# Where the combined weights are made and when the fourth batch's loads are queued, in a one-core attention and mixture kernel

## The chip, the cores and the metric

The kernel runs on one core of a Trainium2 chip. The metric is the device time of one execution in microseconds (us), lower is better. Engines are called as in the profile: PE is TensorE's matrix multiply and PEld its weight load, DVE is VectorE, ACT is ScalarE, POOL is GpSimd, and SP is SyncE, whose queue issues every DMA of this kernel.

## What is computed

Four batches of 576 tokens go through a block-causal attention with 8 heads of 64, then through a first network, in which the largest of three products is taken per element, then through four experts whose outputs are weighted by shares and added:

```python
attn = softmax(where(block_i >= block_j, q @ k.T / 8, -1e9)) @ v       # 4 x 8 heads x 576 x 64
x = attn as 2304 tokens x 512
h = max(max(x @ w1, x @ w2), x @ w3)                                   # 512 -> 768
x = h @ w_out                                                          # 768 -> 512
p = domain_probs / sum(domain_probs)                                   # 2304 x 4, the shares
out = sum over e of p[:, e] * (relu(x @ w1[e]) @ w2[e])                # 512 -> 1024 -> 512
```

Each product is made of three matmuls on pairs of a rounded value and its remainder, so that it is near float32.

## The kernel before, in words

**Order of the work.** The attention runs over 16 pairs of heads, four pairs to a batch. The first network of batches 0, 1 and 2 (`moe1`, L545) is a generator that the class `Filler` (L686) steps in between the steps of the attention of the batch behind it: so many of its matmuls are put behind each attention step. When the attention ends, 15 or 16 steps of batch 2's network are left. Then come batch 3's network in another form (`moe1_last`, L577) and the experts (from L1351).

**First network.** `moe1` takes 18 weight tiles (`order`, L551; three weight matrices, six tiles of 128 hidden columns each), 12 matmuls for each, into one PSUM bank; ACT (L560) or DVE (L562) evicts it. Its second layer, `moe1_out` (L535), runs over four output tiles d; each needs a weight tile "wo" of 768 KB that `moe_weight` (L462, DMA at L475) loads from `held`, where batch 0 left the weights as pairs. There are two buffers of "wo", so the tile of d = 2 can come only when the matmuls of d = 0 are over, and that of d = 3 when those of d = 1 are.

**Combined weights.** Batch 3 forms each product of 2 x 2 blocks from seven block products instead of eight, nine groups of seven (`moe1_last`, L597 to 681). Four of the seven need sums of weight blocks. These are made ahead by `sums` (L517), in batches 1 and 2, as soon as both tiles of a group have been used: two additions (L523), four more (L525 to 528), a rounded copy on ACT (L529), a difference (L530), all in a part of `arena` as scratch, and a DMA of 1 MB to `summed[g]` (L531). Groups 0 to 3 are made in batch 1, groups 4 to 8 in batch 2 (`SHARE = 4`), all in the same part of `arena`, that of batch 2's outputs: a group's first addition waits for the store of the group before. `moe1_last` loads them (L611) into the tiles "xh", "xl" and two buffers of "w1", in turn. The "w1" buffers lie where the attention's tiles lay.

**Shares.** Twelve small DMAs (L794 four, L802 eight) load the expert shares into `pr`, four small DVE instructions (L804 to 807) make `prt` of them. They stand in the code right behind the end of the attention. `keep_in_program_order` queues each of them behind the SP instruction that stands before it in the code.

**Expert weights.** `weights_in(e, n)` (L960) loads raw first-layer weights into the one scratch tile "t" (L968), combines them on DVE (L936) and splits them into pairs on ACT and DVE (L944) in a buffer of "w1". `combine` (L841) uses the same "t" for the token blocks. `save_tails` (L880) stores token blocks (L885) for a later pass.

**What sets the order.** Code order is not queue order. The framework's planner simulates the engines and each queue, and puts into a queue what its simulation holds for ready, the earlier in the code the sooner. On the chip each queue then runs strictly in that order: an instruction that waits holds up all behind it. `tc.issue_after(ins)` adds an edge for what is traced within it and runs on the same engine as `ins`: it is queued behind `ins`, and doesn't wait for its end.

The end of the stage, in code order (L1292 to 1309):

```python
    filler.work.append(moe1_last(xc))
    for _ in following:
        filler.upto(filler.done + 1)
    while begun[0] < NGRP - 1:
        filler.upto(filler.done + 1)
    ready = [weights_in(0, 0)]
    filler.upto(filler.done + 8)
    following = combine(*blocks(0))
...
    ready.append(weights_in(0, 1))
    filler.rest()
    save_tails()
```

Of the kernel before, what the change touches and what calls it, by code (L numbers as in the profile page):

```python
# [7 lines left out]
F32R = mybir.dt.float32r  # L8
# [4 lines left out]
ALU = mybir.AluOpType  # L13
AX = mybir.AxisListType
# [3 lines left out]
RAWS = 3  # L18

WT = 5  # L20
SHARE = 4
FROM = 8
P = 128

# [4 lines left out]
def program(tc, q, k, v, w123, w_out, probs, e_w1, e_w2, out):  # L29
    nc = tc.nc  # L30

    B, H, D, S = k.shape[0], 2 * k.shape[1], k.shape[2] // 2, k.shape[3]
    NT, DM = out.shape
    FF = w_out.shape[2] // 2
    E, F2 = e_w1.shape[0], 2 * P * e_w1.shape[1]
    KD = DM // P
    NF = FF // P
    NPAIR = H // 2
    NTT = NT // P
# [4 lines left out]
    def f(ap):  # L44
        return ap.bitcast(F32)
# [5 lines left out]
    prs = const.tile([P, NTT], F32, name="prs")  # L51
# [3 lines left out]
    prt = const.tile([P, E, NTT], F32, name="prt")  # L55
# [10 lines left out]
    summed = [dram.tile([P, 2, 4, 2 * P], F32, name=f"summed{i}") for i in range(3 * NF // 2)]  # L66
# [18 lines left out]
    CT, KH = 384, KD // 2  # L85
# [12 lines left out]
    pairs, later, made, exps, normal, least = {}, [], {}, [], [], []  # L98
# [363 lines left out]
    def moe_weight(b, n, at=0, a0=0):  # L462

        if b == 0:
            return convert.weight(n)
        A = tiles[n].shape[1]
        wide = n >= 3 * NF
        if b == B - 1 and not wide:
            if at == 0:
                taken[0] = 0  # L470
            if at % WT >= 3:
                wide = True
                taken[0] += 1
        wt = weight_tile(n, wide)
        nc.sync.dma_start(  # L475
            out=f(wt[:, :, a0:A].rearrange("p k a f -> p k (a f)")), in_=held[n][:, :, a0 * P:A * P]
        )
        return wt
# [37 lines left out]

    def sums(g, w0, w1):  # L517

        o = 2 * KD * S
        high, raw = (arena[:, o + i * 8 * P:o + (i + 1) * 8 * P] for i in range(2))  # L520
        for i, w in enumerate((w0, w1)):
            x = [w[:, j].rearrange("p a f -> p (a f)") for j in range(2)]
            nc.vector.tensor_tensor(raw[:, i * 4 * P:(i + 1) * 4 * P], f(x[0]), f(x[1]), op=ALU.add)  # L523
        a11, a12, a21, a22 = (raw[:, i * 2 * P:(i + 1) * 2 * P] for i in range(4))
        nc.vector.tensor_tensor(a22, a21, a22, op=ALU.add)  # L525
        nc.vector.tensor_tensor(a21, a11, a21, op=ALU.subtract)
        nc.vector.tensor_tensor(a11, a22, a11, op=ALU.subtract)
        nc.vector.tensor_tensor(a12, a12, a11, op=ALU.subtract)
        nc.scalar.copy(high.bitcast(F32R), raw)  # L529
        nc.vector.tensor_tensor(raw.bitcast(F32R), raw, high, op=ALU.subtract)  # L530
        nc.sync.dma_start(  # L531
            out=summed[g].rearrange("p x s f -> p (x s f)"), in_=arena[:, o:o + 16 * P]
        )

    def moe1_out(b, runs):  # L535
        for d in range(KD):
            wt = moe_weight(b, 3 * NF + d)
            for w, hh, hl, to in runs:
                m = ps_m.tile([P, 512], F32, name="m", tag="m")[:, 0:w]
                yield from mm3(m, [(wt[:, 0, ff], wt[:, 1, ff], hh[ff], hl[ff]) for ff in range(NF)])  # L540
                x = to(d)
                nc.scalar.copy(x, m if len(x.shape) == 2 else m.rearrange("p (b s) -> p b s", b=B))
                yield

    def moe1(b):  # L545
        hidden = [mp.tile([P, NF, MAIN], F32R, name=x, tag=x) for x in ("hh", "hl")]
        hh, hl = ([x[:, ff] for ff in range(NF)] for x in hidden)
        xh, xl = xs[b]
        prev, last = {}, {}
        if b:  # L550
            order = [(2 * j + i, n) for j in range(NF // 2) for n in range(3) for i in range(2)]  # L551
        else:
            order = [(ff, n) for ff in range(NF) for n in range(3)]
        for at, (ff, n) in enumerate(order):
            wt = moe_weight(b, 3 * ff + n, at)
            m = ps_m.tile([P, 512], F32, name="m", tag="m")[:, 0:MAIN]
            yield from mm3(m, [(wt[:, 0, d], wt[:, 1, d], xh[:, d], xl[:, d]) for d in range(KD)])
            if n == 0:
                prev[ff] = mp.tile([P, MAIN], F32, name="mt", tag="mt", bufs=3)
                nc.scalar.copy(prev[ff], m)  # L560
            else:
                nc.vector.tensor_tensor(prev[ff], m, prev[ff], op=ALU.max)  # L562
            t = prev[ff]
            if n == 2:
                nc.gpsimd.tensor_scalar(hh[ff], t, 1.0, 0.0, op0=ALU.mult, op1=ALU.add)
                nc.gpsimd.tensor_tensor(hl[ff], t, f(hh[ff]), op=ALU.subtract)
            if b and ff % 2:
                g = 3 * (ff // 2) + n
                if (g >= SHARE) == (b > 1):
                    sums(g, last[0], wt)  # L570
            last[0] = wt
            yield
        yield from moe1_out(b, [(MAIN, hh, hl, lambda d: x2f[b][:, d, 0:MAIN])])

    begun = [0]

    def moe1_last(xc):  # L577

        b = B - 1
# [13 lines left out]
            nc.vector.tensor_tensor(to, x, y, op=ALU.add)  # L593
            return to

        at = 0
        for j in range(NF // 2):  # L597
            state = {}
            for n in range(3):
                begun[0] += 1  # L600
                w0 = moe_weight(b, 6 * j + n, at)
                w1 = moe_weight(b, 6 * j + 3 + n, at + 1, KH)
                at += 2
                tag = ("xh", "xl", "w1", "w1")[(3 * j + n) % 4]
# [3 lines left out]
                else:  # L608
                    w2 = mp.tile([P, KD, MAIN], F32R, name=tag, tag=tag).rearrange("p d (s f) -> p (d s) f", s=2)
                w2 = w2.rearrange("p (x s) f -> p x s f", x=2)  # L610
                nc.sync.dma_start(  # L611
                    out=f(w2).rearrange("p x s f -> p (x s f)"),
                    in_=summed[3 * j + n].rearrange("p x s f -> p (x s f)"),
                )

                def side(name, x, k):
                    if name in TERMS:
# [85 lines left out]
    filler = Filler()  # L703
# [24 lines left out]
    for n in range(NALL):  # L728
        b, d = divmod(n, NPAIR)
# [45 lines left out]
    def rows(p, c, t):  # L775
        if p < NPASS - 1:
            return [(0, (2 * p + c) * S + t * P, P)]
        found, at = [], t * P
        while at < (t + 1) * P:
            b, s = divmod(at, TAIL)  # L780
            n = min((t + 1) * P - at, TAIL - s)
            found.append((at - t * P, (2 * c + b) * S + CT + s, n))
            at += n
        return found

    def tile_of(p, c, t):
        return (2 * p + c) * TPC + t

    pr = xp.tile([P, NTT, E], F32, name="pr", tag="pr")
    for p in range(NPASS):  # L790
        for c in range(2):
            if p < NPASS - 1:
                r0 = (2 * p + c) * S
                tc.keep_in_program_order(nc.sync.dma_start(  # L794
                    out=pr[:, tile_of(p, c, 0):tile_of(p, c, TPC)],
                    in_=probs[r0:r0 + CT].rearrange("(t p) e -> p t e", p=P),
                ))
                continue
            for t in range(TPC):
                for a, r, n in rows(p, c, t):  # L800
                    tc.keep_in_program_order(
                        nc.sync.dma_start(out=pr[a:a + n, tile_of(p, c, t)], in_=probs[r:r + n])  # L802
                    )
    nc.vector.tensor_reduce(prs, pr, axis=AX.X, op=ALU.add)  # L804
    nc.vector.tensor_scalar(prs, prs, 1e-9, None, op0=ALU.add)
    nc.vector.reciprocal(prs, prs)
    nc.vector.tensor_tensor(
        prt.rearrange("x e t -> x t e"), pr, prs[:].unsqueeze(2).to_broadcast([P, NTT, E]), op=ALU.mult
    )
    shares = dram.tile([E * NTT, P], F32, name="shares")  # L810

    def split(dst_h, dst_l, raw, low):
# [67 lines left out]
    def save_tails():  # L880
        for d in range(2):
            for c in range(2):
                x = tokens(NPASS - 1, c, d)
                for k in range(KH):
                    nc.sync.dma_start(out=tails[d][c][:, k], in_=x[:, k])  # L885
# [71 lines left out]
    def load(out_, in_):  # L957
        loads.append(nc.sync.dma_start(out=out_, in_=in_))

    def weights_in(e, n):  # L960

        w = xp.tile([P, 7, 2, QW_], F32R, name="w1", tag="w1", bufs=2)
        if (e, n) in stored:
            load(f(w[:]), kept1[e][n][:])
            return w
        stored.add((e, n))
        raw = scratch()[:, 0:7 * QW_].rearrange("x (n f) -> x n f", n=7)
        nc.sync.dma_start(out=raw[:, 0:4], in_=e_w1[e, n])  # L968
        combos(*(raw[:, i] for i in (0, 1, 2, 3, 4, 5, 6, 3)))
        halves(w, raw, [(nc.vector, 0, 4), (nc.vector, 4, 7)])  # L970
        nc.sync.dma_start(out=kept1[e][n][:], in_=f(w[:]))
        return w
# [321 lines left out]
    filler.work.append(moe1_last(xc))  # L1294
    for _ in following:
        filler.upto(filler.done + 1)
    while begun[0] < NGRP - 1:
        filler.upto(filler.done + 1)
    ready = [weights_in(0, 0)]
    filler.upto(filler.done + 8)  # L1300
    following = combine(*blocks(0))
    xc = next(following)
    for _ in following:
        filler.upto(filler.done + 3)
    ready.append(weights_in(0, 1))
    filler.rest()
    save_tails()
    moe.close()
    ps.close()
# [180 lines left out]
```

## Time and profile before

| what | value |
|---|---|
| time, median of 3 runs | 1244.34 us (1242.67 to 1246.34) |
| time of the profiled execution | 1241.92 us |
| its span, first to last instruction | 1240.1 us |
| PE busy | 1191.9 us, 96% of the span |
| DVE, ACT, POOL busy | 903.8, 486.0, 283.4 us |
| attention with batches 0 to 2 | from 0 to about 391 us |
| batch 3's network, its second layer to the end | about 412 to 512 us |
| experts | 512 to 1240 us |

A row of the timeline has the start, the duration, the engine and line, what it writes and reads, and in brackets how long its engine was idle before it and what ended that. A window's row has for each engine the busy time and the number of instructions, then PE's granted clock (1.00 is 2.4 GHz, 0.50 is 1.2 GHz), the busy share of the DMA engines and GB/s. "SPq" rows are DMAs as SP issues them; the time from issue to landing is told separately.

### The profile page before, as it was taken

The page shows a single profiled execution, that of the slowest core. Times are in us where ns is not written, and L with a number is a line of the kernel's source. Part 1 is how long each engine was busy: PE and PEld are TensorE (multiplying, and loading weights), DVE is VectorE, ACT ScalarE, POOL GpSimd, SP SyncE. Part 2 cuts the span into 40 slices and gives each one's busy share as a digit, 9 for nine tenths or more (in the row PEclk, how much of TensorE's full clock was granted, in tenths as well). Part 3 has the DMA queues.
Part 4 walks back from the last instruction along what each step waited for, and adds up shares of the span by engine and source line. Part 5 has one row for each costly group of instructions (what it writes and reads, how often), then busy time and mean ns, then how long its engine had stood idle before and what let it go on. Part 6 is the DMA issues. An engine that isn't in the chain of part 4 may idle for free.

```text
span 1240.1 us, 18286 instructions
## 1 busy us (share of the span) xinstructions
PE 1191.9 (96%) x6887; PEld 1069.8 (86%) x6887; DVE 903.8 (73%) x1570; ACT 486.0 (39%) x1008; POOL 283.4 (23%) x300
## 2 busy tenths in 40 slices
PE   7889999999997998999999999999999999999998
PEld 4567777777775897889999998999999999999998
DVE  4877876554665467598888896758787888686896
ACT  5976664445335123344444450233232223322232
POOL 2459754433332000233333341000000000000000
PEclk8999999999999899899999999999999999999999
DMA  5846766744556564788888865867888887766754
GB/s 207 278 139 218 249 205 215 237 144 138 164 179 218 182 213 160 269 314 320 311 320 303 302 236 175 309 253 314 317 304 310 315 314 280 255 256 232 254 204 178
DMA packets 84652, 303.51 MB, mean 245 GB/s; under 512 B 8973, under 2 KB 20565, under 8 KB 69461
## 3 DMA queue, kind: packets, MB, share of 16 engines
q1 hardware_dynamic: 84564, 302.35, 68.5%
q8 instruction: 54, 0.88, 0.3%
q14 instruction: 34, 0.27, 0.1%
HBM read 209.75 MB, written 92.57 MB: 244 GB/s over the span
## 4 chain that ended last, share of the span: by engine, by line
PE 66%; DVE 14%; DMA 11%; ACT 5%; issue 2%; POOL 1%; SPq 0%; DVEq 0%; ACTq 0%; POOLq 0%
PE m L993 20%; PE o L1152 17%; PE m L489 13%; PE m L625 5%; DMA t<-in_e_w 4%; PE tt L286 2%; PE pv L321 2%; PE st L188 2%; DMA summed<-arena 2%; ACT p L232 2%; PE m L1152 2%; DVE w L948 2%; DVE hl L1054 2%; DMA part<-in_e_w 1%; DVE tmp L1013 1%
## 5 line engine op out<-in xcount | busy, mean ns | idle before, releaser
L993 PE MATMUL m<-t,w 128*128 128x384 f32 x1152 | 227.9, 336 | 1.3 <-DVE w L948 1.3
L1152 PE MATMUL o<-hx,w 128*128 128x384 f32 x1176 | 226.1, 337 | 0.5 <-DMA w<-kb 0.5
L1152 PEld LDWEIGHTS o<-hx,w 128*128 128x128 f32 x1176 | 207.9, 188 | 0.8 <-PE m L993 0.8
L993 PEld LDWEIGHTS m<-t,w 128*128 128x128 f32 x1152 | 203.4, 188 | 4.2 <-DVE w L948 1.6
L993 PE MATMUL m<-b,w 128*128 128x384 f32 x864 | 175.4, 336 | 1.5 <-ACT tmp L1018 1.5
L993 PEld LDWEIGHTS m<-b,w 128*128 128x128 f32 x864 | 153.1, 188 | 4.9 <-ACT tmp L1018 1.8
L232 ACT ACTIVATE p<-st,mn 128x128 f32<-128x128 f32 (+2 forms) x144 | 78.7, 557 | 71.6 <-DVE mn L225 71.3
L258 POOL TENSOR_SCALAR p<-p,sm 128x128 f32<-128x128 f32 (+4 forms) x108 | 78.0, 737 | 103.9 <-ACT high L126 51.2
L948 POOL TENSOR_TENSOR w<-part,w 128x512 fp32r<-128x512 f32 x32 | 50.1, 1587 | 192.5 <-ACT w L946 192.4
L1013 DVE TENSOR_TENSOR tmp<-m,tmp 128x384 f32<-128x384 f32 x144 | 77.5, 550 | 17.3 <-PE m L993 14.6
L489 PE MATMUL m<-xh,wt 128*128 128x512 f32 x256 | 85.6, 399 | 0.0
L489 PE MATMUL m<-hh,wo 128*128 128x512 f32 x192 | 67.5, 419 | 13.7 <-DMA wo<-held 12.1
L1123 ACT CAST hx<-hq 128x768 fp32r<-128x768 f32 x49 | 40.6, 837 | 99.0 <-PE o L1152 76.1
L225 DVE TENSOR_REDUCE mn<-st 128x1 f32<-128x128 f32 (+2 forms) x144 | 68.1, 512 | 15.3 <-ACT p L232 7.3
L286 PE MATMUL tt<-ident,p 128*128 128x128 f32 x400 | 62.7, 289 | 15.1 <-ACT eh L296 6.6
L1079 PE MATMUL o<-w,hl 128*128 128x512 f32 x192 | 74.7, 391 | 0.0
L1078 PE MATMUL o<-w,hh 128*128 128x512 f32 x192 | 74.6, 390 | 0.0
L1075 PE MATMUL o<-w,hh 128*128 128x512 f32 x192 | 74.3, 391 | 0.0
L286 PEld LDWEIGHTS tt<-ident,p 128*128 128x128 f32 x400 | 48.0, 147 | 29.8 <-ACT eh L296 8.2
L948 POOL TENSOR_TENSOR part<-mix,part 128x512 fp32r<-128x512 f32 x32 | 44.1, 1385 | 75.7 <-ACT part L946 75.7
L1123 ACT CAST hx<-part 128x768 fp32r<-128x768 f32 x28 | 23.3, 836 | 91.4 <-PE o L1152 69.4
L489 PEld LDWEIGHTS m<-hh,wo 128*128 128x128 f32 x192 | 38.0, 200 | 24.1 <-issue 6.8
(225 smaller groups left out, 2275.6 us busy)
## 6 DMA issues: line engine op xcount, KB each, us to landing
w<-kb SPq DMA_DIRECT2D x55, 1024.0 KB, 5.9
w<-ka SPq DMA_DIRECT2D x28, 1792.0 KB, 7.6
ka<-w SPq DMA_DIRECT2D x16, 1792.0 KB, 6.7
kb<-part SPq DMA_DIRECT2D x16, 1024.0 KB, 6.6
wt<-held SPq DMA_DIRECT2D x28, 512.0 KB, 4.7
kb<-w SPq DMA_DIRECT2D x16, 768.0 KB, 5.5
arena<-in_w SPq DMA_DIRECT2D x18, 512.0 KB, 4.6
wo<-held SPq DMA_DIRECT2D x12, 768.0 KB, 5.5
```

The lines of the kernel that those rows point to most:

```text
L225: least.append(nc.vector.tensor_reduce(mn[:, m:m + 1], x, axis=AX.X, op=ALU.min))
L232: exps.append(nc.scalar.activation(to, x, ACTF.Exp, bias=mn[:, m:m + 1], scale=-1.0, accum_out=sm[:, m:m + 1],))
L258: normal.append(nc.gpsimd.tensor_scalar(x, x, sm[:, c:c + 1], 1.0, op0=ALU.mult, op1=ALU.mult))
L286: nc.tensor.transpose(tt[:, c:c + P], pt[i][:, k0:k0 + P], ident)
L489: nc.tensor.matmul(out=out_, lhsT=w, rhs=x, start=m == 0, stop=m == n - 1)
L948: eng.tensor_tensor(w[:, a:b, 1], raw[:, a:b], f(w[:, a:b, 0]), op=ALU.subtract)
L993: ins = nc.tensor.matmul(out=m, lhsT=a, rhs=b, start=start and n == 0, stop=stop and n == 3 * KH - 1, skip_group_check=True,)
L1013: nc.vector.tensor_tensor(t, x, y, op=ALU.add)
L1075: ins = nc.tensor.matmul(out=o, lhsT=hh[:, ts], rhs=wh, start=i == 0, stop=False)
L1078: nc.tensor.matmul(out=o, lhsT=hh[:, ts], rhs=wl, start=False, stop=False)
L1079: nc.tensor.matmul(out=o, lhsT=hl[:, ts], rhs=wh, start=False, stop=i == G - 1)
L1152: nc.tensor.matmul(out=o, lhsT=a, rhs=b, start=start and m == 0, stop=stop and m == 2, skip_group_check=True,)
```

## The change

Four things. `sums` makes the even groups in batch 1 (five: 0, 2, 4, 6, 8) and the odd ones in batch 2 (four), and groups 2 and 6 use another part of `arena`, that of batch 1's outputs. `sums` becomes a generator in two halves: the additions come where they came, and the copy, the difference and the store are traced behind the next weight tile's eviction, the copy under `issue_after` of it. The loads of combined weights into "w1" are queued behind the last weight load of batch 2 (`made["load"]`, its fourth "wo"). The loads of the shares are traced once six groups of batch 3 have begun, and queued behind the sixth group's load of combined weights; the first load of expert weights is queued behind the last such load traced by then (the eighth group's), and the second, `weights_in(0, 1)`, is traced behind all of batch 3 and queued behind its last "wo" load.

```diff
-SHARE = 4
...
         wt = weight_tile(n, wide)
-        nc.sync.dma_start(
+        made["load"] = nc.sync.dma_start(
...
     def sums(g, w0, w1):
 
-        o = 2 * KD * S
+        o = (2 - (g // 2 % 2) * (g % 2 == 0)) * KD * S
...
-        nc.scalar.copy(high.bitcast(F32R), raw)
+        behind = yield
+        with tc.issue_after(behind.ins):
+            nc.scalar.copy(high.bitcast(F32R), raw)
         nc.vector.tensor_tensor(raw.bitcast(F32R), raw, high, op=ALU.subtract)
         nc.sync.dma_start(
             out=summed[g].rearrange("p x s f -> p (x s f)"), in_=arena[:, o:o + 16 * P]
         )
+        yield
...
             if n == 0:
                 prev[ff] = mp.tile([P, MAIN], F32, name="mt", tag="mt", bufs=3)
-                nc.scalar.copy(prev[ff], m)
+                ins = nc.scalar.copy(prev[ff], m)
             else:
-                nc.vector.tensor_tensor(prev[ff], m, prev[ff], op=ALU.max)
+                ins = nc.vector.tensor_tensor(prev[ff], m, prev[ff], op=ALU.max)
+            if under:
+                under.pop().send(ins)
...
             if b and ff % 2:
                 g = 3 * (ff // 2) + n
-                if (g >= SHARE) == (b > 1):
-                    sums(g, last[0], wt)
+                if g % 2 == b - 1:
+                    under.append(sums(g, last[0], wt))
+                    next(under[0])
             last[0] = wt
             yield
+        for x in under:
+            x.send(ins)
...
-        at = 0
+        at, behind = 0, made["load"]
...
-                nc.sync.dma_start(
-                    out=f(w2).rearrange("p x s f -> p (x s f)"),
-                    in_=summed[3 * j + n].rearrange("p x s f -> p (x s f)"),
-                )
+                with tc.issue_after(behind.ins) if tag == "w1" else nullcontext():
+                    made["sums"] = nc.sync.dma_start(
+                        out=f(w2).rearrange("p x s f -> p (x s f)"),
+                        in_=summed[3 * j + n].rearrange("p x s f -> p (x s f)"),
+                    )
...
+    def load_shares():
+        for p in range(NPASS):
...
+        nc.vector.tensor_reduce(prs, pr, axis=AX.X, op=ALU.add)
...
-    def weights_in(e, n):
+    def weights_in(e, n, behind=None):
...
-        nc.sync.dma_start(out=raw[:, 0:4], in_=e_w1[e, n])
+        with tc.issue_after(behind.ins) if behind else nullcontext():
+            nc.sync.dma_start(out=raw[:, 0:4], in_=e_w1[e, n])
...
+    while begun[0] < 6:
+        filler.upto(filler.done + 1)
+    with tc.issue_after(made["sums"].ins):
+        load_shares()
     while begun[0] < NGRP - 1:
         filler.upto(filler.done + 1)
-    ready = [weights_in(0, 0)]
+    ready = [weights_in(0, 0, made["sums"])]
...
-    ready.append(weights_in(0, 1))
     filler.rest()
+    ready.append(weights_in(0, 1, made["load"]))
     save_tails()
```

`load_shares` holds the loops and the four DVE instructions of L790 to 809 unchanged.

## Rows read from the trace of the kernel before

**Rows 1.** Windows: engines' busy time (instructions), granted clock, DMA share, GB/s.

```profile
core 0: us, PE busy (x) PEld busy (x) DVE busy (x) ACT busy (x) POOL busy (x), PEclk, DMA share, GB/s
...
202.40:205.80 3.40, 3.40 (x9) 2.67 (x8) 2.04 (x1) 0.65 (x2) 2.49 (x2) 0.50 0.35 96
206.00:232.00 26.00, 25.98 (x166) 20.23 (x166) 17.61 (x39) 10.71 (x29) 7.94 (x9) 1.00 0.67 228
...
326.00:379.00 53.00, 48.65 (x288) 37.46 (x286) 37.30 (x81) 21.58 (x58) 20.77 (x23) 1.00 0.61 216
399.60:403.80 4.20, 0.00 (x0) 0.00 (x0) 1.91 (x6) 1.42 (x2) 0.00 (x0) 1.00 0.37 84
403.80:410.60 6.80, 4.83 (x11) 3.80 (x12) 2.23 (x5) 0.00 (x0) 0.00 (x0) 0.50 0.51 181
492.30:495.90 3.60, 0.00 (x0) 0.00 (x0) 1.31 (x4) 0.69 (x3) 0.00 (x0) 1.00 0.96 350
495.90:502.80 6.90, 5.42 (x13) 4.26 (x14) 2.30 (x3) 1.69 (x2) 0.00 (x0) 0.51 1.03 410
512.00:530.00 18.00, 18.00 (x106) 17.68 (x105) 15.10 (x21) 9.21 (x17) 9.76 (x7) 1.00 0.72 257
```

**Rows 2.** Timeline of PE, 200 to 500 us.

```profile
201.39 0.50 PE L489 MATMUL m<-xh,wu 128*128 128x512 f32 x1 [1.87 <-ACT mt L560]
...
395.11 0.62 PE L489 MATMUL m<-hh,wo 128*128 128x512 f32 x2
...
405.77 0.77 PE L489 MATMUL m<-hh,wo 128*128 128x512 f32 x1 [6.20 <-DMA wo<-held]
...
436.25 1.20 PE L625 MATMUL m<-b,wo 128*128 128x384 f32 x6
...
497.38 0.80 PE L489 MATMUL m<-hh,wo 128*128 128x512 f32 x1 [5.13 <-DMA wo<-held]
```

**Rows 3.** Queue of SP: DMAs as they are issued, 391 to 500 us.

```profile
391.11 0.81 SPq L611 DMA_DIRECT2D w<-summed  x2
391.97 3.55 SPq L794 DMA_DIRECT2D pr<-in_probs  x4
395.57 5.63 SPq L802 DMA_DIRECT2D pr<-in_probs  x8
401.31 1.03 SPq L475 DMA_DIRECT2D wo<-held  x2
...
427.73 0.33 SPq L611 DMA_DIRECT2D xl<-summed  x1
430.18 2.60 SPq L475 DMA_DIRECT2D wo<-held  x2
...
490.13 0.33 SPq L968 DMA_DIRECT2D t<-in_e_w  x1
...
491.82 1.01 SPq L475 DMA_DIRECT2D wo<-held  x2
```

**Rows 4.** Chain of work that ended last, in order of time: start, us, what.

```profile
401.31 4.33 DMA wo<-held
...
491.82 5.52 DMA wo<-held
```

**Rows 5.** Time from issue to landing of the "wo" loads, 290 to 520 us.

```profile
DMA to landing us min/median/max: 3.8/4.7/10.9
```

**Rows 6.** SP's waits, 463 to 516 us: total, times, longest.

```profile
SPq L475 <- PE m L489: 0.5, 1, 0.5
```

**Rows 7.** Timeline of DVE: the sums of group 1, and weights of expert 0.

```profile
193.90 1.29 DVE L523 TENSOR_TENSOR arena<-wu 128x512 f32<-128x512 f32 x2 [3.80 <-DMA summed<-arena]
...
496.89 2.09 DVE L948 TENSOR_TENSOR w<-t,w 128x1024 fp32r<-128x1024 f32 x2 [0.78 <-ACT w L946]
```

**Rows 8.** Waits, 180 to 405 us: total, times, longest.

```profile
DVE arena L523 <- DMA summed<-arena: 17.4, 7, 4.2
...
ACT arena L529 <- DVE arena L528: 24.1, 5, 8.3
```

More of the change, by code (lines that the diff above doesn't have):

```diff
@@ L548, in moe1 @@
         xh, xl = xs[b]
-        prev, last = {}, {}
+        prev, last, under = {}, {}, []
         if b:
@@ L789, in program @@
     pr = xp.tile([P, NTT, E], F32, name="pr", tag="pr")
[L790 to L809, printed above, removed]
+    def load_shares():
+        for p in range(NPASS):
+            for c in range(2):
+                if p < NPASS - 1:
+                    r0 = (2 * p + c) * S
+                    tc.keep_in_program_order(nc.sync.dma_start(
+                        out=pr[:, tile_of(p, c, 0):tile_of(p, c, TPC)],
+                        in_=probs[r0:r0 + CT].rearrange("(t p) e -> p t e", p=P),
+                    ))
+                    continue
+                for t in range(TPC):
+                    for a, r, n in rows(p, c, t):
+                        tc.keep_in_program_order(
+                            nc.sync.dma_start(out=pr[a:a + n, tile_of(p, c, t)], in_=probs[r:r + n])
+                        )
+        nc.vector.tensor_reduce(prs, pr, axis=AX.X, op=ALU.add)
+        nc.vector.tensor_scalar(prs, prs, 1e-9, None, op0=ALU.add)
+        nc.vector.reciprocal(prs, prs)
+        nc.vector.tensor_tensor(
+            prt.rearrange("x e t -> x t e"), pr, prs[:].unsqueeze(2).to_broadcast([P, NTT, E]), op=ALU.mult
+        )
     shares = dram.tile([E * NTT, P], F32, name="shares")
```

## The prediction

> **What bounds the kernel now.** I read first the windows, stage by stage: PE is the engine that is full nearly everywhere (25.98 of 26 us from 206 to 232, 18.00 of 18 from 512), so a change pays only where PE is idle or its clock is low. In the stages touched the windows show three such places [rows 1]. From 399.6 PE does nothing for 4.2 us and then runs at a granted clock of 0.50 (1.2 GHz) until 410.6. From 492.3 to 495.9 it does nothing again, then runs at 0.51 until 502.8. From 202.4 to 205.8 it runs at 0.50. And between 326 and 379 it is busy 48.65 of 53.00 us.
>
> PE's timeline says what each idle stretch waited for [rows 2]: 6.20 us before 405.77 and 5.13 us before 497.38 for a "wo" weight tile, 1.87 us before 201.39 for an ACT eviction. SP's queue tells why the first tile was late [rows 3]: two "w" loads at 391.11, then twelve loads of shares from 391.97 to 401.2, and only then "wo", at 401.31. Its buffer was free much earlier: the matmuls of the tile before it ended with the first one of the pair at 395.11, at about 395.5 [rows 2]. So the wait is SP's own order. The chain of waits carries both loads, 4.33 and 5.52 us [rows 4].
>
> **The second layer of batch 2.** The shares leave this place, and the "w" loads are queued behind the "wo" load. Then "wo" can be issued at 395.5 instead of 401.31. It lands 4.33 us later [rows 4], the other landings lying between 3.8 and 10.9 [rows 5]; I take 4.33, the same load at the same place, with now less ahead of it. That gives 399.9, and PE is done with its other work at 405.77 - 6.20 = 399.57. Of the 6.20 us some 0.4 remain. The half clock goes too: PE was busy 4.83 us at 0.50 [rows 1], of which 2.4 were lost. Gain 6.2 + 2.4 - 0.4 = **8.2 us**. Bounds: with the slowest landing (10.9) 1.6, with the fastest 8.6. Nothing else is late next that I see: the products behind have their operands, whose last preparation on DVE stood behind the shares' own loads.
>
> **The second layer of batch 3.** The load of expert weights at 490.13 (512 KB) moves behind the two "wo" loads at 491.82 [rows 3]. But SP was not what held these: its only wait for PE there is 0.5 us [rows 6], it was there when the buffer came free. So the issue time stays; only the landing can shrink, from 5.52 to the 4.33 of the load with little traffic beside it [rows 4]: 1.2 us. The clock had fallen 3.6 us after the last matmul here and 4.2 us after it in the other place [rows 1]; an idle stretch of 5.1 - 1.2 = 3.9 us lies between these, so I count no gain from it. Gain **1.2 us**; bounds 0 (same landing) and 1.2 + 2.7, half of the 5.42 us at 0.51 [rows 1], if the clock holds.
>
> **The sums in batch 1.** Group 1 goes to batch 2, and group 2 uses another buffer. DVE waited 3.80 us at 193.90 for group 0's store before it began group 1 [rows 7]; behind it stood the reductions that ACT's exponentials wait for, behind these the eviction that PE waited for at 201.39 [rows 2]. That wait goes: 1.87 us, and of the 3.40 us at 0.50 [rows 1] half, 1.7. Gain **3.6 us**; bounds 0, if group 0's second half, now behind an eviction, gets in the same way, and 3.6. The batch has one group more to make (five, not four). From 206 to 232, where two groups were made within 26 us with such waits, PE lost 0.02 us [rows 1], so I cost the further ones at nothing; their cover is the matmuls of batch 1, and the rival below prices its failing.
>
> **The sums in batch 2.** Four groups instead of five, every fourth weight tile instead of every second, so the store of one is over before the next begins. DVE's waits for such stores are 17.4 us in seven times over both batches, ACT's waits for DVE's additions 24.1 us in five [rows 8]. PE's idle time from 326 to 379 is 53.00 - 48.65 = 4.35 us [rows 1]. I take 3.0 of it, as the rest is the attention's own chain; bounds 0 and 4.35. The moved copy costs ACT nothing new, it is the same copy later; SP's stores move with it, to places where no load was waiting long.
>
> **The shares.** Their twelve issues fall behind the sixth load of combined weights, at 427.73 in the old times [rows 3]. Behind them in the queue is the "wo" load of the fifth group, free at 430.18, first used at 436.25 [rows 2, 3]; landing at 4.7 [rows 5], it has about 1.4 us to spare. The planner looks at each load when it is ready, so some four shares go ahead of it and delay it by part of one issue. I take 0.3; bounds 0 and, if all twelve go first, 427.73 + 0.33 + 9.2 + 0.3 + 4.7 = 442.2, a PE wait of 6.0 us and half a clock behind it as at 405.77, 2.4: 8.4. DVE's four instructions take under 1 us where DVE has room.
>
> **The expert weights.** The first load goes behind the eighth sums load; its buffer came free later than that anyway. The second lands about 5 us later, and with it the difference at 496.89 [rows 7]. These weights serve the second seven products of the experts: the first take 42 of the 106 matmuls that fill 18.00 us from 512 [rows 1], so until 519. From 499 + 5 to 519 leaves 15 us. But the scratch tile and the third load go 5 us later too. I take 0.5; bounds 0 and 5.
>
> A page of the Trainium skill speaks against these two moves: DMA: Bandwidth & Descriptors, Rules for kernel authors, wants a DMA issued early and its semaphore waited for late. By it the full 5 us would be lost, and the sum below would come to 1231.2. By the trace the issue that matters is one that something waits for, and the shares were early and cost 6.2 us to the tile behind them.
>
> **Sum.** 8.2 + 1.2 + 3.6 + 3.0 - 0.3 - 0.5 = 15.2 us. The profiled execution took 1241.92 us, which gives 1226.7. The median of the runs is 2.4 us above it; the sum from that is 1229.1. I say **1228**. About 0.3%, 3.7 us, is what a measurement of this kernel can tell from no change. The forecast's own range is 1222 to 1234.
>
> **Rivals.** *The shares block the group's weights.* All twelve are queued ahead of the fifth group's "wo": 8.4 us instead of 0.3, so 1234.8. For it: only about 1.4 us to spare. Against: before, they stood ahead because they stood earlier in the code, and now they stand behind that load. Chance 0.10.
>
> *The sums wait elsewhere.* The order behind the eviction binds only where that eviction is ACT's: issue order holds on one engine, and two of three evictions are DVE's. Then ACT still waits for DVE's additions, PE gains nothing in batches 1 and 2 and keeps 15.2 - 6.6 = 8.6: 1233.3. For it: the 24.1 us of such waits [rows 8]. Against: longer distances leave less to wait for. Chance 0.12.
>
> *Late expert weights.* PE waits for them once at the start of the experts, 5 us: 1231.2. Chance 0.03, as 15 us lie between.
>
> *Slower: the extra sums stop the attention.* Five groups in batch 1, each additions and difference on DVE in front of the reductions, each costing PE what group 1 did at 201.39, 3.6 us. That stretch has no idle time now, so it is all loss: four more such stops are 14.4 us, the one of before stays, batch 2 gains nothing. From 8.2 + 1.2 - 0.8 = 8.6 us of gain follows a loss of 5.8: 1247.7. It decides from the third stop on. For it: one such stop is in the trace. Against: it needed the wait for a store, and the two groups after it, with waits, cost nothing. Chance 0.10.
>
> *It doesn't do what it says.* The "wo" load of batch 2 is again not first in the queue, as another load is held for ready there, and the gain of 8.2 falls to about 1, with the sums' gain lost to the planner's new order: 1240 to 1244. Chance 0.08. Against: an edge now holds the "w" loads behind it.
>
> **How the numbers follow.** The forecast has 0.57, the rivals 0.10, 0.12, 0.03, 0.10 and 0.08. Faster by over 0.3% (below 1240.6): 0.57 + 0.10 + 0.12 + 0.03 = 0.82. Within: 0.08. Slower: 0.10. The last two rivals are 0.18, left out, so the range ends at 1240; below, the clock at 497 (2.7), all of 4.35 in batch 2 and the two small costs at zero would add 4.9 to the sum of the profile, 1221.8, and with the new planning order something more: 1219.
>
> **What would show it.** In the profile of after: "wo" issued at about PE's end of the tile before it, with no loads of shares around it, and no window at 0.50 near 400; the wait before batch 3's third "wo" still there, about 4 us; no wait of DVE for a store of sums; no gap before the eviction near 200; PE idle under 1.5 us where it had 4.35; the shares scattered among loads of batch 3 with PE full. Wrong would make it: a PE wait for "wo" in the fifth group, new gaps in batch 1, or PE waiting for expert weights after 512.

## The result, and the profile after

The changed kernel takes 1229.25 us (median of four runs, 1227.60 to 1229.60); the kernel before, run beside it, 1243.51 (1241.37 to 1246.34). The ratio is 0.9881, 95% interval 0.9858 to 0.9904: faster by 1.2%, against 1228 forecast. The profiled execution took 1227.60 us with a span of 1225.8.

Where the time went is read from four points that every version's PE timeline has: a wait for a converted "wo" in batch 0, the attention's last wait in batch 2, the first of batch 3's products, and the experts' first. Of the kernel before:

```profile
172.41 0.50 PE L489 MATMUL m<-hh,wo 128*128 128x512 f32 x1 [0.88 <-ACT wo L101]
388.23 0.87 PE L321 MATMUL pv<-eh,vraw 128*64 128x384 f32 x4 [0.73 <-ACT eh L296]
412.23 1.22 PE L625 MATMUL m<-b,wt 128*128 128x384 f32 x6
512.51 1.21 PE L993 MATMUL m<-b,w 128*128 128x384 f32 x6
```

Of the changed kernel, the same points and, between them, its long waits, which answer to [rows 2]:

```profile
171.44 0.50 PE L488 MATMUL m<-hh,wo 128*128 128x512 f32 x1 [0.88 <-ACT wo L100]
213.42 1.09 PE L285 MATMUL tt<-ident,p 128*128 128x128 f32 x8 [1.22 <-POOL p L257]
282.07 0.56 PE L488 MATMUL m<-hh,wo 128*128 128x512 f32 x1 [4.19 <-DMA wo<-held]
383.69 0.87 PE L320 MATMUL pv<-eh,vraw 128*64 128x384 f32 x4 [0.73 <-ACT eh L295]
395.25 0.50 PE L488 MATMUL m<-hh,wo 128*128 128x512 f32 x1 [0.21 <-DMA wo<-held]
399.49 1.21 PE L633 MATMUL m<-b,wt 128*128 128x384 f32 x6
482.86 0.80 PE L488 MATMUL m<-hh,wo 128*128 128x512 f32 x1 [4.55 <-DMA wo<-held]
497.50 1.21 PE L1004 MATMUL m<-b,w 128*128 128x384 f32 x6
505.24 0.51 PE L1086 MATMUL o<-w,hh 128*128 128x512 f32 x1 [1.19 <-ACT w L956]
506.88 1.35 PE L1004 MATMUL m<-t,w 128*128 128x384 f32 x5 [1.13 <-DVE tmp L1024]
```

The stop at 201.39 [rows 2] has no counterpart, and of the 6.20 us before 405.77 there are 0.21 left, before 395.25. One of 4.19 us at 282.07 is new, and so are two small ones in batch 1, that at 213.42 and one of 0.87 us at 242.06. The points cut each span into five stages, and each stage's length is a difference of two rows (the last ends with the span). Gains over the kernel before, in us, one profiled execution each:

| stage | length before | forecast | changed kernel |
|---|---|---|---|
| 1, to batch 0's "wo" | 172.41 | 0 | 1.0 |
| 2, sums beside the attention | 215.82 | 6.6 | 3.6 |
| 3, second layer of batch 2 | 24.00 | 8.2 | 8.2 |
| 4, batch 3 | 100.28 | 1.2 - 0.3 | 2.3 |
| 5, experts | 727.59 | -0.5 | -0.7 |

Stage 1 has the same code in every version and is 168.83 to 173.42 us long in the fourteen profiles; its 1.0 is chance, not a gain of the change. Stages 2 to 5 give 13.3 us.

The windows of the changed kernel, which answer to [rows 1]:

```profile
core 0: us, PE busy (x) PEld busy (x) DVE busy (x) ACT busy (x) POOL busy (x), PEclk, DMA share, GB/s
277.80:282.10 4.30, 0.11 (x2) 0.04 (x1) 1.33 (x3) 4.30 (x13) 1.78 (x3) 1.00 1.00 332
282.10:285.80 3.70, 3.70 (x9) 2.89 (x10) 0.00 (x0) 0.05 (x1) 2.01 (x3) 0.54 0.33 136
322.00:374.00 52.00, 52.00 (x346) 41.20 (x344) 31.60 (x71) 23.49 (x65) 20.85 (x28) 1.00 0.50 169
396.00:406.00 10.00, 10.00 (x54) 9.34 (x54) 2.08 (x3) 2.57 (x5) 0.00 (x0) 1.00 0.59 226
482.90:487.20 4.30, 4.30 (x10) 3.43 (x11) 0.25 (x1) 0.00 (x0) 0.00 (x0) 0.50 0.90 290
500.00:512.00 12.00, 9.67 (x45) 8.98 (x44) 10.25 (x17) 6.11 (x11) 5.68 (x4) 0.86 0.58 197
```

Where PE was idle for 4.35 us from 326 to 379, its counterpart is full, 52.00 of 52. The half clock near 400 is gone (1.00 from 396), that after batch 3's wait is still there (0.50), and a third has come at 282 (0.54), behind the new wait.

The chain of waits has three "wo" loads now, the first of them new (the others answer to [rows 4]):

```profile
275.77 6.25 DMA wo<-held
...
390.99 4.21 DMA wo<-held
...
478.10 4.71 DMA wo<-held
```

SP's queue in batch 3, answering to the shares of [rows 3]: they go out in portions between the other loads, and "wo" gets its place among them.

```profile
415.34 2.03 SPq L803 DMA_DIRECT2D pr<-in_probs  x4
417.46 0.53 SPq L474 DMA_DIRECT2D wo<-held  x1
418.04 2.33 SPq L811 DMA_DIRECT2D pr<-in_probs  x3
420.47 0.56 SPq L474 DMA_DIRECT2D wo<-held  x1
421.07 2.87 SPq L811 DMA_DIRECT2D pr<-in_probs  x5
```

The waits, as in [rows 8]: DVE's for stores of sums no longer appear (17.4 us before); ACT's for DVE's additions are fewer.

```profile
ACT arena L530 <- DVE arena L527: 14.7, 3, 5.6
```

**The new wait.** Group 1 is now batch 2's first group. Its additions need only its two weight tiles, which are loaded ahead, so the planner places them before batch 1's second layer. The timelines of DVE and ACT, in order of time, then SP's queue, then SP's waits there:

```profile
266.60 0.69 DVE L522 TENSOR_TENSOR arena<-wt 128x512 f32<-128x512 f32 x1 [2.80 <-DMA wt<-held]
...
272.96 1.05 ACT L530 CAST arena<-arena 128x1024 fp32r<-128x1024 f32 x1 [4.97 <-DVE arena L527]
...
274.05 1.27 DVE L531 TENSOR_TENSOR arena<-arena 128x1024 fp32r<-128x1024 f32 x1 [0.52 <-ACT arena L530]
```

```profile
266.65 0.33 SPq L114 DMA_DIRECT2D vraw<-in_v  x1
275.35 0.33 SPq L532 DMA_DIRECT2D summed<-arena  x1
275.77 2.45 SPq L474 DMA_DIRECT2D wo<-held  x2
```

```profile
SPq L532 <- DVE arena L531: 8.3, 1, 8.3
```

DVE's additions run from 266.60 to 272.9, with batch 2's inputs in between; ACT's copy waited for them, the difference for the copy, and SP for 8.3 us for the difference, with batch 1's third "wo" next in the queue. This reading was a guess until the third run below.

### The profile page after: what moved, and what is told of

Read it like the earlier page. It is cut to its first block, busy times and chain, and to the rows that moved or that the text cites. A ratio compares the mean times of both kernels' runs of the same rounds, so it can differ in the third digit from the quotient of the medians.

```text
span 1225.8 us, 18284 instructions
## 1 busy us (share of the span) xinstructions
PE 1186.1 (97%) x6887; PEld 1068.0 (87%) x6887; DVE 901.4 (74%) x1570; ACT 486.1 (40%) x1008; POOL 285.3 (23%) x300
## 4 chain that ended last, share of the span: by engine, by line
PE 85%; DMA 5%; ACT 4%; DVE 3%; POOL 2%; issue 1%; SPq 0%; POOLq 0%; DVEq 0%; ACTq 0%
PE m L1004 28%; PE o L1163 17%; PE m L488 14%; PE m L633 5%; PE o L1090 4%; PE o L1089 4%; PE o L1086 4%; PE tt L285 3%; PE st L187 2%; PE pv L320 2%; PE m L1163 2%; ACT p L231 2%; DMA wo<-held 1%; DMA w<-kb 1%; DMA wu<-held 1%
## 5 line engine op out<-in xcount | busy, mean ns | idle before, releaser
L1135 DVE TENSOR_TENSOR hx<-hq,hx 128x768 fp32r<-128x768 f32 x49 | 46.6, 953 | 16.0 <-ACT hx L1134 15.7
```

## The experiments

Twelve versions were timed, 5 to 12 executions of each. The intervals are about 0.2% to either side, some 2.5 us, so smaller differences between versions are read from the stages of the profiles. That is one execution of each version, and not always a typical one: what stages 2 to 5 gain together and what the ratio says differ by 0.4 to 2.5 us, and by 4.8 in one version (store and tails). In the names "t" is the load of raw expert weights, "kb" the store of converted second-layer weights for a later pass, and a room is one of a tile's buffers. Gains over the kernel before, in us:

| version | ratio (95% interval) | stage 2 | 3 | 4 | 5 |
|---|---|---|---|---|---|
| changed kernel | 0.9881 (0.9858 to 0.9904) | 3.6 | 8.2 | 2.3 | -0.7 |
| loads only | 0.9952 (0.9934 to 0.9969) | -0.7 | 8.1 | 2.2 | -3.1 |
| sums only | 0.9967 (0.9951 to 0.9982) | 3.2 | 0.3 | 0.0 | -1.2 |
| group 1's store behind "wo" | 0.9855 (0.9836 to 0.9873) | 9.5 | 8.4 | 2.9 | -1.4 |
| expert weights at the old place | 0.9906 (0.9884 to 0.9927) | 4.2 | 8.1 | -0.4 | -2.3 |
| shares at the old place | 0.9884 (0.9868 to 0.9901) | 3.7 | 8.4 | 1.9 | -1.3 |
| without the w1 edge | 0.9936 (0.9915 to 0.9956) | 1.3 | 7.3 | 2.5 | -5.7 |
| the same, kb behind t | 0.9913 (0.9893 to 0.9933) | 3.6 | 6.8 | 2.7 | -0.9 |
| copy at once | 0.9913 (0.9891 to 0.9935) | 3.1 | 8.2 | 2.3 | -1.3 |
| t behind kb | 0.9900 (0.9883 to 0.9917) | 3.2 | 8.1 | 3.1 | -3.5 |
| store and tails behind "wo" | 0.9837 (0.9817 to 0.9858) | 8.4 | 8.3 | -0.3 | -0.9 |
| store, rooms, kb behind t | 1.0006 (0.9995 to 1.0017) | 9.0 | 8.5 | 6.9 | -24.8 |
| store, rooms, old place | 0.9816 (0.9794 to 0.9839) | 9.1 | 8.4 | 3.0 | 0.6 |

**Each part alone.** The first version keeps the loads' new order and makes the sums as before (undoing the hunks in `sums` and `moe1`); the second is the kernel before with just those hunks.

```diff
-                if g % 2 == b - 1:
-                    under.append(sums(g, last[0], wt))
-                    next(under[0])
+                if (g >= SHARE) == (b > 1):
+                    sums(g, last[0], wt)
```

> The sums are made as before (groups 0 to 3 in batch 1, the rest in batch 2), the loads are in the new order. Theory A (the two parts add up, each paid where the milestones of the two traces show it): the second layer of batch 2 gives 8.2 us, that of batch 3 about 2.3, the later weights of expert 0 cost about 2.7, so 7.8 us below the kernel before, about 1235.7; the wait on wo at 395 of the kernel before is gone, the stalls between 326 and 388 are still there. Theory B (the loads only pay because the sums no longer hold the second batch up): the gap before wo stays over 3 us and the kernel stands within 3 us of the kernel before, 1240 to 1244.

> The sums are made in the new way, the loads are in the order of before. Theory A: the stop at 201 (3.6 us) and those between 326 and 388 (6.5) go, two small ones at 213 and 242 (2.1) and the new one before wo at 282 (5.9 with the clock) come, so 2 us below the kernel before, about 1241.5; the gap before wo near 395 stays over 5 us. Theory B (the sums carry most of the gain, as the wait on wo at 395 came from the groups made late in batch 2): 8 us or more below, 1235 or less, with the gap near 395 under 2 us.

Measured 1236.93 and 1238.17 us beside 1242.67. Stage by stage theory A holds where the edits are: the loads give stage 3 its 8.1, the sums give stage 2 its 3.2, and neither does the other's work; with the sums alone PE still waits 5.72 us for "wo" at 402.80. By time the parts don't add up: 5.7 and 4.5 us make 10.2 of the 14.3 that the whole gains. The stages are short by 4.6, of which 3.5 lie among the experts (-3.1 and -1.2 against -0.7), where the edits of the loads' version have nothing (below). The sums alone gain 4.5 us, between the 2 of theory A and the 8 of theory B.

**The store in front of "wo".**

```diff
-        nc.sync.dma_start(out=summed[g]...
+        with tc.issue_after(ahead.ins) if ahead else nullcontext():
+            nc.sync.dma_start(out=summed[g]...
...
+        ahead = made["load"] if b > 1 else None    # at the start of moe1(b)
```

> The changed kernel, with the store of the second batch's first group (group 1) queued on SP behind batch 1's two loads of wo. Theory A (the store's wait on the subtraction holds SP's queue, and wo behind it lands late): the gap of 4.2 us at 282 and the half clock behind it go, 5.9 us below the changed kernel, about 1223.3, at least 4 us. Theory B (wo is late since its buffer comes free late or the DMA engines are full): wo is issued at most 1 us earlier, the gap stays over 3 us, and the time is within 1.5 us of the changed kernel's.

Measured 1224.32 us, ratio 0.9855; stage 2 gains 5.9 us more than the changed kernel's. Its queue, and the wait that is left of the 4.19 us:

```profile
273.40 6.48 SPq L474 DMA_DIRECT2D wo<-held  x2
279.98 0.38 SPq L533 DMA_DIRECT2D summed<-arena  x1
```

```profile
285.12 0.47 PE L488 MATMUL m<-hh,wo 128*128 128x512 f32 x1 [0.27 <-DMA wo<-held]
```

Counted from the first point, "wo" leaves at 99.98 instead of 104.33 us, 4.4 earlier. Theory A: the store was the cause of the wait. The medians are 4.9 us apart; the intervals of the two ratios overlap, so it is the queue and the stage that show it.

**Shares or edge?** My working gave the 8.2 us of stage 3 to both moves together. First the shares back where they stood in the program, then, instead, the edge away:

```diff
-    with tc.issue_after(made["sums"].ins):
-        load_shares()
...
+    load_shares()    # right behind its definition
```

```diff
-                with tc.issue_after(behind.ins) if tag == "w1" else nullcontext():
+                with nullcontext():
```

> The changed kernel, with the twelve loads of the shares where the kernel before has them in the program (SP's queue then has them just ahead of batch 2's last load of wo), all else as changed. Theory A (the shares' loads cannot go out before the room that the attention leaves is free at 391, and then 9.2 us of issuing stand ahead of wo): wo is issued near 400, the gap before batch 3 is again 6 us with the half clock behind it, and the time is 7 to 8.5 us above the changed kernel, about 1237. Theory B (they go out in SP's idle stretch between 382 and 391, and what held wo up was only the two loads of sums): wo is issued by 392, within 1 us of the changed kernel.

Measured 1229.32 us, the changed kernel's time. Theory B:

```profile
382.77 0.32 SPq L474 DMA_DIRECT2D wo<-held  x1
383.18 1.98 SPq L803 DMA_DIRECT2D pr<-in_probs  x4
385.21 5.29 SPq L811 DMA_DIRECT2D pr<-in_probs  x8
391.97 0.33 SPq L474 DMA_DIRECT2D wo<-held  x1
```

All twelve go out while SP has nothing else to do, and "wo" leaves as soon as its room is free. In the kernel before they could not, as the two "w" loads ahead of them waited until 391.11 [rows 3]; their 9.2 us of issuing then began too late.

> The changed kernel without the edge that puts the two loads of sums into the room w1 behind the load of wo; SP's queue then has both of them, 1 MB each, ahead of wo. Theory A (what is issued ahead of wo also lands ahead of it): wo is issued 0.8 us later and lands 4 to 6 us later, the gap near 395 grows from 0.2 to 4 us or more with a half clock behind it, and the time is 4 to 7 us above the changed kernel. Theory B (transfers share the DMA engines, only the place in SP's queue counts): 0.8 us, the gap stays under 1.5 us and the time within 1.5 us.

Measured 1234.94 us, so by time theory A; but the gap was that of theory B:

```profile
395.96 0.50 PE L488 MATMUL m<-hh,wo 128*128 128x512 f32 x1 [1.18 <-DMA wo<-held]
...
580.32 2.21 PE L1004 MATMUL m<-t,w 128*128 128x384 f32 x11 [0.94 <-DVE tmp L1024]
...
595.11 0.50 PE L1086 MATMUL o<-w,hh 128*128 128x512 f32 x1 [1.55 <-DVE arena L1096]
```

SP has the two "w" loads out at 386.31 and "wo" at 390.74: without the shares in between the waiting head doesn't keep "wo" from going out either. Stage 3 lost 0.9 us. Stage 2 lost 2.2 and stage 5 lost 5.0, where the edit has nothing. In stage 5 SP's queue has the store "kb" of expert 0's third second-layer weights ahead of the load "t" of expert 1's first, as in the version with the loads alone; in all versions until then that lose less than 2.5 us in stage 5, "t" is first. Two versions put an order in by hand: the version without the edge with that store behind the load, and the changed kernel with the load behind the store.

```diff
+        behind = stores[0, 2] if (e, n) == (1, 0) else behind    # the second; the first holds the store back
         with tc.issue_after(behind.ins) if behind else nullcontext():
             nc.sync.dma_start(out=raw[:, 0:4], in_=e_w1[e, n])
```

> The version without the w1 edge, with that store of kb queued behind the load of t, as the changed kernel has them. Theory A (the edge itself is worth the 1.2 us gap near 395, the other 4 to 5 us of its 5.7 were the swap): about 1230.5, at most 2.5 us above the changed kernel. Theory B (the edge is worth all of it): 4 us or more above, as without this.

> The changed kernel with one edge more: the load of expert 1's first raw weights (t) is queued on SP behind the store of expert 0's third second-layer weights (kb), as the plan has it in the version with the loads alone and in the one without the w1 edge; the plan of the changed kernel has t first. Theory A (this swap in the plan, far from the edit, is what these two versions lose between 500 and 620): 3 to 5 us above the changed kernel, about 1233.3, with new gaps of about 1 us and 1.5 us between 575 and 600. Theory B (the loss comes from something else in them): within 1 us of the changed kernel.

Measured 1233.41 and 1231.29 us. The first is 4.2 us above the changed kernel: by time theory B, and not clear of the version that it is made from (1234.94). Its profile, of its fastest execution (1228.85), speaks for theory A: stage 5 loses 0.9 instead of 5.7, and stage 3 still gains 6.8. The swap in the changed kernel comes out between its theories, 2.0 us above by the medians with overlapping intervals; its profile loses 2.8 us more in stage 5, not at 575 to 600, where only 0.35 us came, but by a wait of 1.64 us at 736.44 among others. So the swap may take part in the loss; that it causes it is not shown, and what else in the plan does stays open. The edge itself is worth 0.9 to 1.4 us of stage 3.

**The copy behind the eviction.**

```diff
-        behind = yield
-        with tc.issue_after(behind.ins):
-            nc.scalar.copy(high.bitcast(F32R), raw)
+        nc.scalar.copy(high.bitcast(F32R), raw)
+        behind = yield
```

> The changed kernel, with ACT's copy of the sums made at once, not behind the next eviction. Theory A (the copy waits in ACT's queue for DVE's additions and holds the evictions behind it, which is what stopped PE at 201 in the kernel before): stops of 1 to 2 us come back at several of the nine groups, 3 us or more above the changed kernel. Theory B (the even and odd split alone took the stops away, as each batch has fewer of the groups that met an eviction): within 1.5 us of the changed kernel.

Measured 1232.80 us, ratio 0.9913: by the medians theory A, just (3.6 us above, with overlapping intervals). Its stops did not come back as theory A has them, though: PE has none near 201. So the stop of the kernel before went with the new split, group 1 no longer waiting there for group 0's store, and not with the deferred copy. Stage 2 gains 3.1 instead of 3.6, with the wait for "wo" down from 4.19 to 0.61 us, as group 1's store left at 273.61, before the tile's room came free and "wo" followed at 275.97. Other stops took its place, the last with a granted clock of 0.55 behind it (380.60 to 383.00):

```profile
280.97 0.50 PE L488 MATMUL m<-hh,wo 128*128 128x512 f32 x1 [0.61 <-DMA wo<-held]
...
300.59 1.09 PE L285 MATMUL tt<-ident,p 128*128 128x128 f32 x8 [0.69 <-POOL p L257]
...
380.67 1.64 PE L285 MATMUL tt<-ident,p 128*128 128x128 f32 x7 [2.07 <-POOL p L257]
```

Against the version whose store is out of the way, 9.5, the deferred copy would be worth some 6 us of stage 2. That is an estimate from two single profiles; no version has the copy at once and the store behind "wo".

**The later expert weights.**

```diff
+    ready.append(weights_in(0, 1))
     filler.rest()
-    ready.append(weights_in(0, 1, made["load"]))
```

> The changed kernel, with the load of expert 0's second weights at its place of before (ahead of batch 3's second layer's last steps and of wo). Theory A (the later load is what stops the experts at 505 and 507): the two gaps of 1.2 us and the half clock behind them go, 2.7 back, of which the longer landing of wo at 480 takes up to 1.1: 1.2 to 2.7 us below the changed kernel, about 1227. Theory B (those gaps come from the order in which ACT and DVE convert, not from the load): the gaps stay and the time is the changed kernel's or up to 1.5 us above it.

Measured 1230.57 us, ratio 0.9906: theory B's time, for another reason (1.3 us above the changed kernel, inside the intervals). The gaps at 505 and 507 do go, but batch 3's wait is longer:

```profile
481.93 0.79 PE L488 MATMUL m<-hh,wo 128*128 128x512 f32 x1 [5.91 <-DMA wo<-held]
...
526.93 2.71 PE L1004 MATMUL m<-t,w 128*128 128x384 f32 x14 [1.25 <-DVE w L958]
```

5.91 instead of 4.55 us, with more half clock behind it: stage 4 gains 2.7 us less, and one gap of 1.25 us among the experts follows, as in the kernel before (1.33 us at 542.19). By the stages the move pays where batch 3 ends, and the 2.3 us of stage 4 are its own: the version with the loads alone has 2.2 of them, that with the sums alone none.

**Batch 3's wait.** This one the change left in place, as forecast; with the store out of the way it is the longest. Two stores of the tails, which wait for ACT, stand ahead of the third "wo". The first run puts the eight stores behind the last "wo":

```diff
+                    with tc.issue_after(made["load"].ins):
                         nc.sync.dma_start(out=tails[d][c][:, k], in_=x[:, k])
```

> The version with group 1's store behind batch 1's wo, and also the eight stores of the fourth batch's tails behind the last load of wo. Theory A (the first two of these stores wait for ACT's eviction and stand ahead of the third load of wo): wo is issued about 1.3 us earlier and the gap of 4.2 us at 478 shrinks by as much, 1 to 2.5 us below the version with the store alone, about 1222.5. Theory B (wo waits for its own room, freed at the same time): nothing, within 0.7 us of it, 1224.3.

Measured 1223.93 us, within 0.4 us of the version it is made from, and the wait is 3.98 us instead of 4.18: theory B. (Its stage 4 also has a stop of 2.02 us at 428.98 for a "wt" tile, with a granted clock of 0.67 over the next 4 us.) So the stores don't hold it. Whether the tile's room does, the next two test; they load that third "wo" in two pieces into rooms of "wt":

```diff
+            if b == B - 1 and d == 2:
+                pair = [mp.tile([P, 2, KD, P], F32R, name="wt", tag="wt", bufs=3) for _ in range(2)]
+                for x, a, z in zip(pair, (0, KD), (KD, NF)):
+                    nc.sync.dma_start(... held[n][:, :, a * P:z * P])
```

> The version with group 1's store behind batch 1's wo; batch 3's third wo is loaded in two pieces into two rooms of wt, which the first layer has done with, and every early store of kb is queued behind the load of t two groups on. Theory A (wo's two rooms are what makes PE wait at 478): the gap of 4.2 us and most of the half clock behind it go, 4 to 7 us below the version with the store alone, about 1219. Theory B (the rooms of wt come free no sooner, or the wait goes over to the fourth wo or to the experts' first weights): within 2 us of it.

Measured 1243.76 us, as slow as before. Both theories were short of it. The wait of 4.18 us for the third "wo" went, 1.57 us for the fourth came, and stage 4 gained 4 us more, as theory A has it: it was the room. But the experts lost 24.8. From 560 to 740 PE waited where the largest groups of the version with the store alone have no idle time; this is one of three that do here:

```profile
L1024 PE MATMUL m<-b,w 128*128 128x384 f32 x195 | 42.2, 341 | 4.8 <-ACT w L968 2.6 <-ACT tmp L1049 2.1
```

Of the 23.4 us that the experts lose against that version 13.8 are idle time of PE, nearly all before 800. With every "kb" held back by hand the plan is worse there; which of these edges does it was not tried. Without them, and with the expert weights at their old place:

> The version with group 1's store behind batch 1's wo and batch 3's third wo in two rooms of wt, now without the moved stores of kb, and with the load of expert 0's second weights at its place of before; SP's plan among the experts is the changed kernel's again. Theory A (the rooms take 2.6 us or more off the wait at 478, as in the run before, and what that run lost among the experts came with its plan there): 4 to 6 us below the version with the store alone, about 1219, with no loss of more than 2 us between 500 and 800. Theory B (with batch 3's end earlier the experts' conversions are the next bound, whatever the plan): the gain at 478 is given back by 620 and the time is within 2 us of that version or above it.

Measured **1219.71 us**, ratio 0.9816 (0.9794 to 0.9839): by time theory A, and the fastest version, below both kernels. Its queue and waits:

```profile
457.97 3.52 SPq L544 DMA_DIRECT2D wt<-held  x2
```

```profile
427.22 1.28 PE L645 MATMUL m<-b,wt 128*128 128x384 f32 x6 [2.14 <-DMA wt<-held]
...
482.94 0.47 PE L488 MATMUL m<-hh,wo 128*128 128x512 f32 x1 [1.90 <-DMA wo<-held]
```

The third tile's loads go out from 457.97 and its first matmul comes at 469.40 without a wait; the fourth is now the one waited for, 1.90 us. The experts lose nothing (0.6 gained). The 4.6 us below the version with the store alone are not shown to come from the room: stage 4 gains 3.0 against 2.9 there, as a stop of 2.14 us at 427.22 took back what the room gave (without it, by estimate, near 5); stage 5 gives 1.9 and stage 1, whose code is the same, 2.2. And two things changed from the run before, the "kb" edges and the place of the expert weights; no run parts them.

## Why the prediction was right, and where its steps failed

That the total was right is in part luck. The sums came out 3.0 us short of their forecast, one gain in them too small and one loss left out; batch 3, with 1.4 us more than its 0.9, and the start of the kernel, with 1.0 of chance, gave most of it back.

- **Second layer of batch 2**: 8.2 forecast, 8.2 measured, with the half clock gone as worked out and "wo" landing in 4.21 us against 4.33 taken. The reason was half right. I read the twelve shares as what held the tile up. They took the time, but only because the head of the queue, the two "w" loads that waited until 391.11, kept them from going out earlier: with the shares at the old place behind no such head, "wo" is not late. It took both; either of the two moves alone gives 6.8 to 8.4 us.
- **The sums**: 3.6 + 3.0 forecast, 3.6 measured, and this is the step that failed, twice. The gain was 9.5 us, not 6.6 (third run): all of the 4.35 us in batch 2 went instead of 3.0, and so did the two stops of 1.38 and 0.74 us behind 379, outside the window I had counted. With the stop at 201 and its half clock these make 10.0 us; stops that are longer or new in that run, 0.97 us the longest, take back 2.4; 1.8 us I can't place. Against it stands a loss of 5.9 us that I put at nothing in one clause, without looking at the order of the queue: SP's stores move "to places where no load was waiting long". One moved in front of batch 1's "wo" and waited there 8.3 us.
- **Second layer of batch 3**: 1.2 forecast, 2.3 measured, inside its bounds. The wait shrank by 0.58 us, the half clock is shorter, and the small wait at 473.93 of the kernel before, 0.77 us, went. The step mis-sized these last two, which it put at nothing.
- **The shares** (-0.3): nothing measurable. They interleave as forecast.
- **Expert weights** (-0.5): stage 5 lost 0.7. The late load is felt, by 1.19 and 1.13 us at 505 and 507, where I had given it 15 us of room. What PE waited for there was not those weights but a copy on ACT and an eviction on DVE; both waits are gone with the load at its old place. By the stages, taking it back cost more than it gave.

The rivals: the shares did not block the fifth group. The sums do wait elsewhere, but PE gained in both batches all the same; what the order behind an eviction is worth there, some 6 us, is the estimate above. The slower case, stops from extra sums in batch 1, came as 1.22 and 0.87 us at 213 and 242, not 3.6 each. Of the signs that I had named for being wrong, two came, both small: these gaps, and PE waiting near the start of the experts. No rival named a store that holds SP.

The rule that I weighed, of the Trainium skill (DMA: Bandwidth & Descriptors, Rules for kernel authors), is to issue a DMA early and to wait on it late. The trace differs here: with the expert load issued earlier, stages 4 and 5 together lose 4.3 us (2.7 and 1.6) against the changed kernel, in one profile each. The times, 1230.57 and 1229.25 us, can't tell the two apart, and the fastest version has that load early too.

## What to carry to other kernels

On a queue that issues in order, look for what its head waits for, not only at what stands last before the load you miss: taking away either the waiting head or the crowd behind it can free the load. When work is moved earlier, follow its last instruction too; a store that waits is a wait for every load behind it. And compare versions by points that their timelines share, stage by stage: here it showed a cancelled loss of 5.9 us that the totals hid, and it separates an edit's effect from that of the new plan far behind it, as far as one execution of each goes.

## What the runs showed that I had not expected

The same code at the start took 168.83 to 173.42 us to the first point, with a mean granted clock between 0.90 and 0.97 over the first 100 us of the profiles. A page of the Trainium skill (TensorE: Matmul & The Clock Gate, Part 1: The HAM clock gate) says that the number of matmuls at the low level varies from run to run for one kernel; no row here counts them, but the clock fits: the three profiles with 0.97 are the three shortest (168.83 to 169.02 us). The spread, 4.6 us, is a third of the effect under study.

A "wt" load in batch 3 was waited for by 2.02 and 2.14 us in two profiles and by nothing in others with the same queue order around it (the version with the store alone issues the same loads in the same order from 410.85 to 425.76). Whether that is the landing alone was not tried.
